# A gated recurrence and its two-layer network: turning the inputs by transposing DMA from DRAM scratch instead of on TensorE, with a set order for every engine

## Chip, cores, metric

One core of one Trainium2 chip. The metric is device microseconds (us) of one execution, median of the fast runs. A run counts as slow when it is over 1.5% above the fastest of the same kernel.

## The reference

```
f = lb + (1 - lb) * sigmoid(f_logit)          # x, f_logit: 4 x 6144 x 256, fp32
h[t] = f[t] * h[t-1] + (1 - f[t]) * x[t]      # per batch and channel, over 6144 tokens
out = max(h @ w1, h @ w2) @ w_out             # w1, w2: 256 x 1024; w_out: 1024 x 256
```

Both kernels use max(a, b) = a + relu(b - a): "hidden" is relu(h @ (w2 - w1)), and "project" adds h @ (w1 @ w_out), whose weights (w13) are made once. They work on 48 blocks of 512 tokens, 12 to a batch. The recurrence runs over tokens along the free dimension, so channels must lie on partitions, while the inputs in DRAM have one token a row. Somebody has to turn them.

## The kernel before

Inputs are cast to bf16 by the GpSimd DMA queue on the way into SBUF, and turned on TensorE (PE), 16 transposes of 128x128 a block, spread over the slots of the loop.

```python
for name, src in (("fn", f_logit), ("xn", x)):            # load(c): one or two blocks
    nat = inpool.tile([P, CH // P, D], BF16, name=name)   # inpool: 4 buffers a name
    nc.gpsimd.dma_start(out=nat[:, 0:ni, :],
        in_=src[b, t0 : t0 + nt, :].rearrange("(i p) d -> p i d", p=P))
# ... turn(j, slot): two of these a slot, into PSUM
nc.tensor.transpose(dst[:, h, q * P : (q + 1) * P],
    ins[c][s][:, o * NSB + q, h * P : (h + 1) * P], ident_b[:])
# ... recurrence(j): u = sigmoid(-fT) on ACT; v = u * xT, ff = 1 - (1-lb) u, scan -> y on DVE
# ... the loop
for j in range(NBLK + 1):
    # load(c) of the chunk that starts at block j + 4
    for fc in range(FC):                 # 8 slots
        if j < NBLK:     hidden(j, fc)       # 2 matmuls of 512 columns, relu on ACT
        if j > 0:        project(j - 1, fc)  # 5 matmuls of 256 columns
        if j + 2 < NBLK: turn(j + 2, fc)     # 2 transposes
    if j + 2 < NBLK: recurrence(j + 2)
```

A load of a later chunk needs a free buffer in SBUF, so it waits until an earlier one has been turned.

Of the kernel before, what the change touches and what calls it, by code (L numbers as in the profile page):

```python
# [12 lines left out]
ENG = mybir.EngineType  # L13
P = 128
# [3 lines left out]
def kernel(  # L18
# [9 lines left out]
):  # L28
    nc = tc.nc
# [7 lines left out]
    NSB = TB // P  # L37
    CH = 2 * TB
    assert S % CH == 0
    NBB = S // TB  # L40
    NBLK = B * NBB
    chunks = [(0, 1), (1, 1)] + [(j, 2) for j in range(2, NBLK, 2)]
    home = {j + o: (c, o) for c, (j, n) in enumerate(chunks) for o in range(n)}
# [3 lines left out]
    inpool = ctx.enter_context(tc.tile_pool(name="inp", bufs=4))  # L47
# [4 lines left out]
    ps_t = ctx.enter_context(  # L52
        tc.tile_pool(name="ps_t", bufs=1, space=bass.MemoryType.PSUM)
    )
    ps_d = ctx.enter_context(
        tc.tile_pool(name="ps_d", bufs=3, space=bass.MemoryType.PSUM)
    )
    ps_o = ctx.enter_context(
        tc.tile_pool(name="ps_o", bufs=3, space=bass.MemoryType.PSUM)
    )  # L60

    ident_f = const.tile([P, P], FP32)
    make_identity(nc, ident_f[:])
    ident_b = const.tile([P, P], BF16)
    nc.vector.tensor_copy(out=ident_b[:], in_=ident_f[:])  # L65

# [3 lines left out]
    nc.sync.dma_start(out=lbc[:], in_=lower_bound.rearrange("(h p) -> p h", p=P))  # L70
    nc.vector.tensor_scalar(
        out=om[:], in0=lbc[:], scalar1=-1.0, scalar2=1.0, op0=ALU.mult, op1=ALU.add
    )
    nc.vector.tensor_scalar_add(out=nom[:], in0=lbc[:], scalar1=-1.0)

    ins = {}

    def load(c):
        j, n = chunks[c]
        b, k = divmod(j, NBB)  # L80
        t0, nt = k * TB, n * TB
        ni = nt // P
        tiles = []
        for name, src in (("fn", f_logit), ("xn", x)):
            nat = inpool.tile([P, CH // P, D], BF16, name=name)
            nc.gpsimd.dma_start(  # L86
                out=nat[:, 0:ni, :],
                in_=src[b, t0 : t0 + nt, :].rearrange("(i p) d -> p i d", p=P),
            )
            tiles.append(nat)  # L90
        ins[c] = tiles

    ys = {}
    turned = {}

    def turn(j, slot):
        c, o = home[j]
        s, q = divmod(slot, FC // 2)
        if q == 0:
            turned[j, s] = ps_t.tile([P, KC, TB], BF16, name=("fT", "xT")[s])  # L100
        dst = turned[j, s]
        for h in range(KC):
            nc.tensor.transpose(  # L103
                dst[:, h, q * P : (q + 1) * P],
                ins[c][s][:, o * NSB + q, h * P : (h + 1) * P],
                ident_b[:],
            )

    def recurrence(j):
        fT, xT = turned[j, 0], turned[j, 1]  # L110
        prev = ys.get(j - 1) if j % NBB else None
        u = midpool.tile([P, KC, TB], BF16, name="u")
        nc.scalar.activation(out=u[:], in_=fT[:], func=AF.Sigmoid, scale=-1.0)  # L113
        v = midpool.tile([P, KC, TB], BF16, name="v")
        nc.vector.tensor_tensor(out=v[:], in0=u[:], in1=xT[:], op=ALU.mult)  # L115
        ff = midpool.tile([P, KC, TB], BF16, name="ff")
        y = ypool.tile([P, KC, TB], BF16, name="y")
        for h in range(KC):
            nc.vector.tensor_scalar(  # L119
                out=ff[:, h, :],  # L120
                in0=u[:, h, :],
                scalar1=nom[:, h : h + 1],
                scalar2=1.0,
                op0=ALU.mult,
                op1=ALU.add,
            )
            nc.vector.tensor_tensor_scan(  # L127
                out=y[:, h, :],
                data0=ff[:, h, :],
                data1=v[:, h, :],  # L130
                initial=0.0 if prev is None else prev[:, h, TB - 1 : TB],
                op0=ALU.mult,
                op1=ALU.add,
            )
        ys[j] = y

    def weight_prep():
        w1n = wpool.tile([P, KC, DFF], FP32)
        w2n = wpool.tile([P, KC, DFF], FP32)
        wob = wpool.tile([P, FC, D], BF16)  # L140
        w1b = wpool.tile([P, KC, DFF], BF16)
        wdf = wpool.tile([P, KC, DFF], FP32)
        wd = wpool.tile([P, KC, DFF], BF16)
        for g in range(2):
            cols = slice(g * DFF // 2, (g + 1) * DFF // 2)
            for w, src in ((w1n, moe_w1), (w2n, moe_w2)):
                nc.scalar.dma_start(
                    out=w[:, :, cols],
                    in_=src[:, cols].rearrange("(kc p) f -> p kc f", p=P),
                )  # L150
        nc.gpsimd.dma_start(
            out=wob[:], in_=moe_w_out.rearrange("(fc p) c -> p fc c", p=P)
        )
        for g in range(2):
            cols = slice(g * DFF // 2, (g + 1) * DFF // 2)
            nc.scalar.copy(out=w1b[:, :, cols], in_=w1n[:, :, cols])  # L156
            nc.vector.tensor_tensor(  # L157
                out=wdf[:, :, cols],
                in0=w2n[:, :, cols],
                in1=w1n[:, :, cols],  # L160
                op=ALU.subtract,
            )
            for kc in range(KC):
                nc.vector.tensor_scalar_mul(
                    out=wd[:, kc, cols], in0=wdf[:, kc, cols], scalar1=om[:, kc : kc + 1]
                )
        w1T = wpool.tile([P, FC, D], BF16)
        for kc in range(KC):
            for g in range(FC // 4):
                pt = ps_d.tile([P, TB], BF16, name="dT")  # L170
                for q in range(4):
                    fc = 4 * g + q
                    nc.tensor.transpose(
                        pt[:, q * P : (q + 1) * P],
                        w1b[:, kc, fc * P : (fc + 1) * P],
                        ident_b[:],
                    )
                nc.scalar.copy(
                    out=w1T[:, 4 * g : 4 * g + 4, kc * P : (kc + 1) * P],
                    in_=pt[:].rearrange("p (q d) -> p q d", q=4),  # L180
                )
        w13 = wpool.tile([P, KC, D], BF16)
        for kc in range(KC):
            psw = ps_o.tile([P, 2, D], FP32, name="psO")
            for fc in range(FC):
                nc.tensor.matmul(  # L186
                    psw[:, 0, :],
                    lhsT=w1T[:, fc, kc * P : (kc + 1) * P],
                    rhs=wob[:, fc, :],
                    start=(fc == 0),  # L190
                    stop=(fc == FC - 1),
                )
            nc.scalar.mul(w13[:, kc, :], psw[:, 0, :], om[:, kc : kc + 1])
        return wd, wob, w13
# [3 lines left out]
    def hidden(j, fc):  # L198
        y = ys[j]
        dT = ps_d.tile([P, TB], FP32, name="dT")  # L200
        for kc in range(KC):
            nc.tensor.matmul(  # L202
                dT[:],
                lhsT=wd[:, kc, fc * P : (fc + 1) * P],
                rhs=y[:, kc, :],
                start=(kc == 0),
                stop=(kc == KC - 1),
            )
        rt = rpool.tile([P, TB], BF16, name="rt")
        nc.scalar.activation(out=rt[:], in_=dT[:], func=AF.Relu)  # L210
        rts[j, fc] = rt

    pos = {}

    def project(j, slot):
        i, half = divmod(slot, 2)
        g, r = divmod(i, 2)
        y = ys[j]
        if r == 0 and half == 0:
            pos[j] = ps_o.tile([P, 2, D], FP32, name="psO")  # L220
        ps = pos[j]
        tok = slice(i * P, (i + 1) * P)
        steps = [(y[:, kc, tok], w13[:, kc, :]) for kc in range(KC)]
        steps += [(rts[j, fc][:, tok], wob[:, fc, :]) for fc in range(FC)]
        n = len(steps)
        for s in range(half * n // 2, (half + 1) * n // 2):
# [8 lines left out]
        if r == 1 and half == 1:  # L235
            osb = opool.tile([P, 2, D], FP32, name="osb")
            nc.vector.tensor_copy(out=osb[:], in_=ps[:])  # L237
            r0 = j * TB + 2 * g * P
            nc.sync.dma_start(
                out=out[r0 : r0 + 2 * P, :].rearrange("(r p) d -> p r d", p=P),  # L240
                in_=osb[:],
            )

    started = {c: chunks[c][0] for c in range(len(chunks))}
    ahead = 4
    for c in range(len(chunks)):
        if started[c] < ahead:
            load(c)
    for slot in range(FC):
        turn(0, slot)  # L250
    recurrence(0)
    wd, wob, w13 = weight_prep()
    for slot in range(FC):
        turn(1, slot)
# [45 lines left out]
```

## Time and profile before

| | before |
|---|---|
| time, median | 445.1 us (445.04 to 445.15, 2 runs) |
| span of the profiled run | 443.3 us |
| PE busy | 423.0 us, 95% |
| ACT, DVE busy | 63%, 56% |
| moved by DMA | 53.5 MB, 121 GB/s |

The profile's page gives busy time by engine, then the span in 40 slices (9 is busy at 90% or more; PEclk is the granted TensorE clock in tenths; GB/s is what the DMA engines moved, counted at the destination), the DMA queues, and the chain of waits that ended last.

```profile
PE 423.0 (95%) x3488; PEld 309.8 (70%) x3488; DVE 247.0 (56%) x345; ACT 278.5 (63%) x442; POOL 44.9 (10%) x57
...
PE   0689999999999999999999999999999999999996
...
PEclk9999999999999999999999999999999999999999
...
GB/s 221 198 198 215 138 124 152 83 146 123 94 140 127 91 163 94 123 151 87 146 119 99 140 121 96 163 95 124 149 85 149 120 95 48 72 49 71 57 64 95
...
q0 software_dynamic: 50992, 25.69, 46.1%
q1 hardware_dynamic: 26384, 25.17, 18.4%
...
PE 94%; DMA 4%; POOL 1%; DVE 0%; issue 0%; POOLq 0%
PE psO L227 47%; PE dT L202 37%; PE xT L103 5%; PE fT L103 5%; DMA wob<-in_moe_w_out_dram 4%; POOL fn L86 1%; POOL xn L86 1%; PE psO L186 0%; DVE osb L237 0%; POOL ident_f masks.py:199 0%; POOL ident_f masks.py:197 0%; POOLq masks.py:199 0%
```

PE is the bound: 94% of the chain, of which L103, the transposes, is 10%. q0 is the GpSimd queue with the casting loads.

The timeline (start, duration, engine, line, what) shows what a transpose costs. First a slot in the middle of the run, then two slots at the end, where nothing is left to turn.

```profile
200.17 0.59 PE L202 MATMUL dT<-y,wd 128*128 128x512 bf16 x2
...
201.15 0.27 PE L103 MATMUL xT<-ident_b,xn 128*128 128x128 bf16 x2
...
201.26 0.59 PE L202 MATMUL dT<-y,wd 128*128 128x512 bf16 x2
```

```profile
425.94 0.59 PE L202 MATMUL dT<-y,wd 128*128 128x512 bf16 x2
...
426.91 0.59 PE L202 MATMUL dT<-y,wd 128*128 128x512 bf16 x2
```

The hidden matmuls (L202) come every 1.09 us in the first and every 0.98 us in the second: 8.72 us against 7.83 us for a block of eight slots. PE streams without a gap in both, so turning costs 0.89 us a block on the critical chain.

### The profile page before, as it was taken

The numbers are of one execution on the slowest core, as the hardware profiler recorded it, in microseconds if no ns is written. First come the engines' busy times: TensorE is split into PE (matmuls) and PEld (weight loads), VectorE is DVE, ScalarE is ACT, GpSimd is POOL, SyncE is SP. The second block draws the span as 40 slices with busy tenths as digits, with TensorE's granted clock in tenths as the row PEclk, the third lists the DMA queues.
The fourth block names the chain that finished last, engine by engine and source line by source line (L and its number), as shares of the span: only waits on it lengthen the run. The fifth ranks groups of instructions, "written<-read, shape, count | busy, mean of one in ns | idle before, by whom it ended". The sixth has DMA issues, their size and how long they took to land.

```text
span 443.3 us, 8434 instructions
## 1 busy us (share of the span) xinstructions
PE 423.0 (95%) x3488; PEld 309.8 (70%) x3488; DVE 247.0 (56%) x345; ACT 278.5 (63%) x442; POOL 44.9 (10%) x57
## 2 busy tenths in 40 slices
PE   0689999999999999999999999999999999999996
PEld 0567777777777777777777777777777777777765
DVE  2744665565556546655655565466546655654631
ACT  3666666666666766666666666666766666666661
POOL 6300101001001001010010010010100100000000
PEclk9999999999999999999999999999999999999999
DMA  8999769487487495694874965956948731212112
GB/s 221 198 198 215 138 124 152 83 146 123 94 140 127 91 163 94 123 151 87 146 119 99 140 121 96 163 95 124 149 85 149 120 95 48 72 49 71 57 64 95
DMA packets 78501, 53.49 MB, mean 121 GB/s; under 512 B 2688, under 2 KB 77440, under 8 KB 78464
## 3 DMA queue, kind: packets, MB, share of 16 engines
q0 software_dynamic: 50992, 25.69, 46.1%
q1 hardware_dynamic: 26384, 25.17, 18.4%
q10 hardware_dynamic: 1088, 2.10, 1.5%
q8 instruction: 27, 0.44, 0.4%
q14 instruction: 10, 0.08, 0.1%
HBM read 53.48 MB, written 25.17 MB: 177 GB/s over the span
## 4 chain that ended last, share of the span: by engine, by line
PE 94%; DMA 4%; POOL 1%; DVE 0%; issue 0%; POOLq 0%
PE psO L227 47%; PE dT L202 37%; PE xT L103 5%; PE fT L103 5%; DMA wob<-in_moe_w_out_dram 4%; POOL fn L86 1%; POOL xn L86 1%; PE psO L186 0%; DVE osb L237 0%; POOL ident_f masks.py:199 0%; POOL ident_f masks.py:197 0%; POOLq masks.py:199 0%; POOLq L284 0%
## 5 line engine op out<-in xcount | busy, mean ns | idle before, releaser
L210 ACT ACTIVATE rt<-dT 128x512 bf16<-128x512 f32 x384 | 226.8, 597 | 142.2 <-PE dT L202 142.1
L227 PE MATMUL psO<-wob,rt 128*128 128x256 bf16 x1536 | 229.8, 273 | 0.0
L202 PE MATMUL dT<-y,wd 128*128 128x512 bf16 x768 | 228.2, 379 | 1.1 <-DVE y L127 1.1
L227 PEld LDWEIGHTS <-rt 128*128 128x128 bf16 x1536 | 150.3, 98 | 57.5
L237 DVE COPY osb<-psO 128x512 f32<-128x512 f32 x96 | 66.4, 692 | 152.5 <-PE psO L227 152.5
L127 DVE TENSOR_TENSOR_SCAN y<-ff,y,v 128x512 bf16<-128x512 bf16 x88 | 108.2, 1272 | 1.5
L227 PE MATMUL psO<-w_182,y 128*128 128x256 bf16 x384 | 73.3, 273 | 0.0
L227 PEld LDWEIGHTS <-y 128*128 128x128 bf16 x384 | 37.6, 98 | 44.4
L103 PE MATMUL fT<-ident_b,fn 128*128 128x128 bf16 x384 | 52.2, 221 | 13.4 <-DVE ident_b L65 13.4
L202 PEld LDWEIGHTS <-wd 128*128 128x128 bf16 x768 | 59.6, 98 | 0.9 <-DVE y L127 0.5
L103 PE MATMUL xT<-ident_b,xn 128*128 128x128 bf16 x384 | 52.2, 221 | 0.0
L113 ACT ACTIVATE u<-fT 128x1024 bf16<-128x1024 bf16 x48 | 49.1, 1024 | 4.9 <-PE fT L103 2.3
L103 PEld LDWEIGHTS <-fn 128*128 128x128 bf16 x384 | 37.3, 99 | 19.2 <-DMA fn<-in_f_logit_dram 11.0
L86 POOL DMA_DIRECT2D fn<-in_f_logit_dram x25 | 21.9, 874 | 237.0 <-PE fT L103 174.2
L119 DVE TENSOR_SCALAR ff<-u,nom 128x512 bf16<-128x512 bf16 x96 | 29.9, 354 | 25.6 <-ACT u L113 25.6
L103 PEld LDWEIGHTS <-xn 128*128 128x128 bf16 x384 | 37.4, 99 | 4.8
L115 DVE TENSOR_TENSOR v<-u,xT 128x1024 bf16<-128x1024 bf16 x48 | 32.5, 677 | 3.9 <-PE xT L103 3.9
L86 POOL DMA_DIRECT2D xn<-in_x_dram x25 | 21.6, 866 | 68.2 <-PE dT L202 64.9
L127 DVE TENSOR_TENSOR_SCAN y<-ff,v 128x512 bf16<-128x512 bf16 x8 | 9.4, 1211 | 0.1
L157 DVE TENSOR_TENSOR wdf<-w2n,w1n 128x1024 f32<-128x1024 f32 x2 | 2.5, 1226 | 6.5 <-DMA w2n<-in_moe_w_dram 6.5
L156 ACT CAST w1b<-w1n 128x1024 bf16<-128x1024 f32 x2 | 2.1, 1045 | 4.6 <-DMA w1n<-in_moe_w_dram 4.6
L186 PE MATMUL psO<-wob,w1T 128*128 128x256 bf16 x16 | 1.9, 272 | 1.8 <-DMA wob<-in_moe_w_out_dram 1.8
(18 smaller groups left out, 15.2 us busy)
## 6 DMA issues: line engine op xcount, KB each, us to landing
out_dram<-osb SPq DMA_DIRECT2D x96, 256.0 KB, 2.7
fn<-in_f_logit_dram POOLq DMA_DIRECT2D x23, 512.0 KB, 8.2
xn<-in_x_dram POOLq DMA_DIRECT2D x23, 512.0 KB, 8.4
w1n<-in_moe_w_dram ACTq DMA_DIRECT2D x2, 512.0 KB, 6.2
w2n<-in_moe_w_dram ACTq DMA_DIRECT2D x2, 512.0 KB, 7.4
fn<-in_f_logit_dram POOLq DMA_DIRECT2D x2, 256.0 KB, 10.3
xn<-in_x_dram POOLq DMA_DIRECT2D x2, 256.0 KB, 10.9
wob<-in_moe_w_out_dram POOLq DMA_DIRECT2D x1, 512.0 KB, 17.0
```

The lines of the kernel that those rows point to most:

```text
L86: nc.gpsimd.dma_start(out=nat[:, 0:ni, :], in_=src[b, t0 : t0 + nt, :].rearrange("(i p) d -> p i d", p=P),)
L103: nc.tensor.transpose(dst[:, h, q * P : (q + 1) * P], ins[c][s][:, o * NSB + q, h * P : (h + 1) * P], ident_b[:],)
L113: nc.scalar.activation(out=u[:], in_=fT[:], func=AF.Sigmoid, scale=-1.0)
L115: nc.vector.tensor_tensor(out=v[:], in0=u[:], in1=xT[:], op=ALU.mult)
L119: nc.vector.tensor_scalar(out=ff[:, h, :], in0=u[:, h, :], scalar1=nom[:, h : h + 1], scalar2=1.0, op0=ALU.mult, op1=ALU.add,)
L127: nc.vector.tensor_tensor_scan(out=y[:, h, :], data0=ff[:, h, :], data1=v[:, h, :], initial=0.0 if prev is None else prev[:, h, TB - 1 : T ...
L156: nc.scalar.copy(out=w1b[:, :, cols], in_=w1n[:, :, cols])
L157: nc.vector.tensor_tensor(out=wdf[:, :, cols], in0=w2n[:, :, cols], in1=w1n[:, :, cols], op=ALU.subtract,)
L202: nc.tensor.matmul(dT[:], lhsT=wd[:, kc, fc * P : (fc + 1) * P], rhs=y[:, kc, :], start=(kc == 0), stop=(kc == KC - 1),)
L210: nc.scalar.activation(out=rt[:], in_=dT[:], func=AF.Relu)
L227: nc.tensor.matmul(ps[:, r, :], lhsT=steps[s][0], rhs=steps[s][1], start=(r == 0 and s == 0), stop=(r == 1 and s == n - 1), skip_group_che ...
L237: nc.vector.tensor_copy(out=osb[:], in_=ps[:])
```

## The change

Intent: take the turning off PE. The first 4 blocks are loaded as fp32 on the SP queue, gated with tokens still on partitions, and turned on PE as before. For the other 44, a pair of blocks at a time: GpSimd's queue casts f_logit and x to bf16 into DRAM scratch, and SP's queue loads them with a transposing DMA, channels on partitions. The order of every engine's instructions is set by hand, the weights' preparation is rewritten, and an output tile takes tokens 2p and 2p+1 to partition p, so that a store writes 2 KB runs and projection reads its weights at a step of two.

```diff
-            nc.gpsimd.dma_start(out=nat[:, 0:ni, :], in_=src[b, t0 : t0 + nt, :]...)
+    scratch = tc.tile_pool(name="scratch", bufs=2, space=bass.MemoryType.DRAM)
+    ttpool = tc.tile_pool(name="turned", bufs=3)
+    def cast(c):                                  # c: a pair of blocks
+        for name, src in (("fs", f_logit), ("xs", x)):
+            t = scratch.tile([CB * TB, D], BF16, name=name)
+            nc.gpsimd.dma_start(out=t[:], in_=src[b, k * TB : (k + CB) * TB, :])
+            rows[c].append(t)
+    def turn_dma(c, s):
+        t = ttpool.tile([P, KC, CB * TB], BF16, name=("fT", "xT")[s])
+        nc.sync.dma_start_transpose(out=t[:], in_=rows[c][s][:])
... # opening: direct loads, weights, blocks 0 and 1, with cast(0) and cast(1) in it
+        for j in range(1, NBLK + 1):
+            for fc in range(FC):
+                hidden(j, fc); project(j - 1, fc)              # j = 1 differs
... # blocks 2 and 3: gated, turned on PE, scanned
+                b = j + 2
+                if NP <= b < NBLK:
+                    if fc == 4: gate(b)                        # ACT reads fT
+                    if fc == 5: drive(b), forget and scan      # DVE reads xT
+                if fc == 5 and j % 2 == 1:
+                    c = (j + 3 - NP) // 2
+                    if 0 <= c < NCH:
+                        for s in range(2): turn_dma(c, s)
+                    if c + 2 < NCH:
+                        cast(c + 2)
```

## The prediction

> **What bounds the kernel now.** TensorE. The chain of waits puts 94% of the 443.3 us span on PE: 47% projection matmuls, 37% hidden matmuls, 10% fT and xT transposes. The table by stretches shows PE busy all of 40 to 430 us at clock 1.00. The timeline at 200 us shows hidden, projection and turning matmuls with a period of 1.09 us a slot, 8.72 us a block of eight slots; at 425 us, where nothing is left to turn, the same slots come every 0.98 us, 7.83 us a block. So turning one block costs PE 0.89 us that nothing hides. ACT (63%) and DVE (56%) have slack.
>
> The opening: the first hidden matmul starts at 18.0 us, PE waits 2 us for the cast of w_out (17 us to landing), the steady loop (block 1) starts at 27.2 us. From there 45 x 8.72 + 2 x 7.83 + 4.4 gives 412, as the timeline has it; 4.0 us of copy and last store follow.
>
> **What the change does.**
> - Removes the PE turning of 44 of 48 blocks, about 43 of them in the loop and on the critical chain: 0.89 us each, about 38 us.
> - Adds DMA: per pair of blocks a cast of 2 x 1 MB to scratch and two transposing loads of 512 KB. No trace here shows such a load. The Trainium skill, "DMA: Bandwidth & Descriptors", section Latency and other measured facts, has 261 GB/s for one with a non-contiguous middle dimension; from that, as an estimate, 4 us of data a pair plus some 2 us of latency. A pair has 15.7 us. Casts took 8.4 us to landing with two in flight, stores 2.7 us. DMA share in the steady stretch was 0.7; the opening shows 1.45 reached, so there is room. A load is issued about 7 us before its sigmoid; five PSUM buffers for hidden let PE run about 4 us past a late ACT.
> - Stores become 2 KB runs; projection's weights are read at a step of two. 40 weight loads a block hide behind 109 ns matmuls (transposes show loads every 56 ns): I expect no cost.
> - Opening: block 0 lands as fp32 near 6 us, its scans end near 10, hidden(0) starts at 11, but w_out (fp32, behind 3 MB, then cast on POOL) gates w13 near 18, and block 1's gate sits behind that: scan(1) ends near 26. Half of block 0's projection is done by then.
>
> **Sum (estimate).** Block 1's loop starts at 26; block 1: 6.6; 1 us wait for scan(2); block 2: 8.7; blocks 3 to 47: 45 x 7.83 = 352; last projection 4.4; tail 4. Span 403, time (1.8 us above the span, as before) 404 us, range 398 to 416. Chances: faster by over 2% 0.93, within 2% 0.04, slower 0.03.
>
> **What would show it.** Slots of 0.98 us from block 4 to the end; PE busy total down by about 40 us, 64 bf16 transposes of inputs instead of 768; projection matmuls still 109 ns apart; chain over 90% PE; transposing loads landing within 7 us; ACT's waits in the loop ended by PE, not DMA; block 1's hidden matmuls starting near 26 us.
>
> **What would make it wrong.** Slow transposing loads: at over about 10 us a pair, sigmoid waits for DMA, PSUM fills and PE stalls each pair; if casts, loads and stores together need over 15.7 us, DMA becomes the bound (430 us or more). Step-two weight loads slower than 109 ns add to 1,920 matmuls, 2 us for each ns. The opening loads may hold back the first cast, stalling around 35 to 50 us.

## The result

| | before | after |
|---|---|---|
| time, median | 445.1 us | 530.0 us (527.75 and 532.25) |
| ratio of fast runs | 1 | 1.1905, 95% interval 1.1785 to 1.2025 |
| span of the profiled run | 443.3 us | 526.0 us |
| PE busy | 423.0 us | 399.5 us |
| mean granted clock | 1.00 | 0.875 |

A ratio here is the mean time of one kernel's fast runs over that of the other's of the same rounds, so it is not quite the ratio of the medians quoted.

The page after, same parts:

```profile
PE 399.5 (76%) x2792; PEld 275.4 (52%) x2792; DVE 247.9 (47%) x343; ACT 273.2 (52%) x444; POOL 27.3 (5%) x54
...
PE   5880200140005999999999999999999999999996
...
PEclk8786555575555999999999999999999999999999
...
GB/s 289 332 210 213 212 251 216 197 91 207 105 57 97 139 160 154 128 109 132 131 151 161 137 116 116 133 140 161 140 119 124 121 141 160 143 139 95 138 70 81
DMA packets 112689, 79.11 MB, mean 150 GB/s; under 512 B 94288, under 2 KB 98384, under 8 KB 111952
...
q1 hardware_dynamic: 110976, 55.59, 44.8%
q0 software_dynamic: 1408, 23.07, 21.9%
...
PE 71%; another core or an unknown queue 23%; ACT 2%; DMA 1%; DVE 1%; issue 1%; SPq 0%; POOL 0%; DVEq 0%; POOLq 0%
```

The PE row has a hole from the fourth slice into the thirteenth and is full after it. The chain gives 23% to "another core or an unknown queue". In order of time, that is two pieces:

```profile
38.13 63.44 another core or an unknown queue
...
105.46 56.67 another core or an unknown queue
```

Between 38 and 164 us the core did almost nothing; from there on it works as forecast. This table by stretches has busy time by engine, then the granted clock, the DMA share and GB/s moved:

```profile
38.00:101.00 63.00, 5.29 (x33) 3.21 (x30) 0.13 (x1) 3.09 (x5) 11.72 (x25) 0.56 1.03 222
101.00:164.00 63.00, 8.41 (x46) 5.15 (x46) 5.04 (x6) 2.44 (x4) 2.92 (x6) 0.55 1.11 122
...
200.00:500.00 300.00, 300.00 (x2150) 210.20 (x2149) 192.15 (x268) 211.37 (x346) 0.00 (x0) 1.00 0.53 136
```

So the question is not why transposing loads are slow. In the steady part they are not: the timeline of the SP queue below has a pair every 15.6 us, and the trace's list by tile gives a median of 4.5 us to landing for fT. What the hole waited for is in the table of waits (engine, line, releaser: total us, times, longest):

```profile
DVE vn L106 <- DMA xn<-in_x_dram: 64.7, 3, 63.5
...
DVE v L186 <- DMA xT<-xs: 57.1, 1, 57.1
ACT u L175 <- DMA fT<-fs: 56.7, 1, 56.7
```

Each is in essence one single wait: x of block 3, a plain load issued at 15.35 us, is used at 101.7 us; then the first transposing load, issued at 30.5, at 162. Here is SP's queue around it and in the steady part:

```profile
15.35 1.41 SPq L89 DMA_DIRECT2D xn<-in_x_dram  x1
...
30.51 113.20 SPq L170 DMA_TRANSPOSE fT<-fs  x1
143.81 15.92 SPq L170 DMA_TRANSPOSE xT<-xs  x1
...
201.72 2.10 SPq L170 DMA_TRANSPOSE fT<-fs  x1
203.91 2.40 SPq L170 DMA_TRANSPOSE xT<-xs  x1
...
217.36 2.02 SPq L170 DMA_TRANSPOSE fT<-fs  x1
```

and this is what GpSimd did meanwhile (the first cast, one on the way, and the last):

```profile
16.30 0.67 POOL L164 DMA_DIRECT2D fs<-in_f_logit_dram  x1
...
40.08 0.49 POOL L164 DMA_DIRECT2D fs<-in_f_logit_dram  x1 [2.03 <-DMA fs<-in_f_logit_dram]
...
126.94 0.49 POOL L164 DMA_DIRECT2D xs<-in_x_dram  x1 [1.98 <-DMA xs<-in_x_dram]
```

All 22 pairs of casts were issued between 16 and 127 us, while the loop, whose pass j = 2 holds both waits above, stood still. In the loop a cast stands after the transposing loads of two pairs before, but that is its place in GpSimd's order alone, and GpSimd has nothing else to do. The built program has no wait for anything but an earlier cast. These are two of its instruction rows for GpSimd (the waits are on the semaphores of the software DMA queue):

```
13 L164 DMACopy fs<-in_f_logit_dram 16x16384
21 L164 DMACopy fs<-in_f_logit_dram 16x16384 [waits DMASW0_49]
```

The pool's "bufs=2" gives no wait either. An SBUF pool hands its buffers out in turn and makes the next writer wait; here no cast waits for the loads that read scratch before, and since kernels with the casts as far ahead as here (e2 and e10 below) give correct results, the scratch tiles do not share memory.

Two more facts. The page's 23.07 MB in 1,408 packets is a mean of 16.4 KB, but no cast packet has that size: only 737 packets of the whole run are 8 KB or larger. The trace's packet records, which the page sums up, have 704 cast packets of 32,768 bytes, 16 to a cast, and 704 of four bytes. (The "16 KB" of the expectations below is this mean.) A plain load has packets of 1 KB and a transposing one of 256 bytes, 2,048 for each of the 44 loads. And between 38 and 101 us the casts, two of 0.52 MB every 5.04 us, moved 208 of the 222 GB/s, which leaves 14 for all else, the loads that everyone waited for among it.

### The profile page after: what moved, and what is told of

Its sections match the earlier page's. It is cut to its first block, busy times and chain, and to the rows that moved or that the text cites. A ratio compares the mean times of both kernels' runs of the same rounds, so it can differ in the third digit from the quotient of the medians.

```text
span 526.0 us, 7133 instructions
## 1 busy us (share of the span) xinstructions
PE 399.5 (76%) x2792; PEld 275.4 (52%) x2792; DVE 247.9 (47%) x343; ACT 273.2 (52%) x444; POOL 27.3 (5%) x54
## 3 DMA queue, kind: packets, MB, share of 16 engines
q0 software_dynamic: 1408, 23.07, 21.9%
## 4 chain that ended last, share of the span: by engine, by line
PE 71%; another core or an unknown queue 23%; ACT 2%; DMA 1%; DVE 1%; issue 1%; SPq 0%; POOL 0%; DVEq 0%; POOLq 0%
PE psO L229 39%; PE dT L200 31%; DMA w2n<-in_moe_w_dram 1%; ACT wd L269 1%; PE dT L118 0%; DVE vn L106 0%; ACT rt L212 0%; SPq L89 0%; POOL wdf L263 0%; PE psO L292 0%; DVE osb L240 0%; DVE y L147 0%; ACT u L175 0%; ACT un L99 0%
## 5 line engine op out<-in xcount | busy, mean ns | idle before, releaser
L212 ACT ACTIVATE rt<-dT 128x512 bf16<-128x512 f32 x380 | 220.9, 596 | 155.9 <-PE dT L200 155.6
L200 PE MATMUL dT<-y,wd 128*128 128x512 bf16 x768 | 232.4, 386 | 4.3 <-DVE y L147 2.2
L186 DVE TENSOR_TENSOR v<-u,xT 128x1024 bf16<-128x1024 bf16 x44 | 30.5, 692 | 116.4 <-ACT u L175 59.3
L200 PEld LDWEIGHTS <-wd 128*128 128x128 bf16 x768 | 75.8, 99 | 17.6 <-issue 4.3
L175 ACT ACTIVATE u<-fT 128x1024 bf16<-128x1024 bf16 x44 | 46.1, 1048 | 56.7 <-DMA fT<-fs 56.7
L229 PE MATMUL psO<-w,y 128*128 128x256 bf16 x384 | 74.1, 275 | 0.0
L106 DVE TENSOR_TENSOR vn<-un,xn 128x1024 bf16<-128x1024 bf16 (+1 forms) x5 | 5.1, 1012 | 68.9 <-DMA xn<-in_x_dram 64.7
L118 PE MATMUL dT<-ident_b,un 128*128 128x128 bf16 x32 | 3.1, 246 | 21.2 <-ACT un L99 21.2
L99 ACT ACTIVATE un<-fn 128x1024 bf16<-128x1024 f32 (+1 forms) x5 | 4.4, 882 | 23.3 <-DMA fn<-in_f_logit_dram 23.3
L164 POOL DMA_DIRECT2D fs<-in_f_logit_dram x22 | 10.9, 495 | 53.7 <-DMA fs<-in_f_logit_dram 53.7
L164 POOL DMA_DIRECT2D xs<-in_x_dram x22 | 10.7, 487 | 35.9 <-DMA xs<-in_x_dram 35.9
L147 DVE TENSOR_TENSOR_SCAN y<-ff,y,dT 128x512 bf16<-128x512 bf16 x6 | 7.4, 1266 | 1.7 <-PE dT L118 1.7
```

The lines of the kernel that those rows point to most:

```text
L106: nc.vector.tensor_tensor(out=vs[j][:, q0:q1, :], in0=us[j][:, q0:q1, :], in1=ins[j][1][:, q0:q1, :], op=ALU.mult,)
L118: nc.tensor.transpose(dst[:, h, q * P : (q + 1) * P], src[:, q, h * P : (h + 1) * P], ident_b[:])
L147: nc.vector.tensor_tensor_scan(out=ys[j][:, h, :], data0=ffs[j][:, h, :], data1=vT[j][:, h, :], initial=0.0 if prev is None else prev[:, h ...
L164: nc.gpsimd.dma_start(out=t[:], in_=src[b, k * TB : (k + CB) * TB, :])
L175: nc.scalar.activation(out=us[j][:], in_=chunk[c, 0][:, :, o * TB : (o + 1) * TB], func=AF.Sigmoid, scale=-1.0,)
L186: nc.vector.tensor_tensor(out=vT[j][:], in0=us[j][:], in1=chunk[c, 1][:, :, o * TB : (o + 1) * TB], op=ALU.mult,)
```

## The experiments

Theory A: the casts run ahead of the loop because nothing holds them, and their large packets leave the loads a small share of each DMA engine. The Trainium skill, "DMA: Bandwidth & Descriptors", section Queues, rings and completion order, says that each engine goes round the queue rows at the granularity of a packet, draining a whole one before it switches. One packet of 1 KB for each cast packet, 16.4 KB in the mean of large and four-byte ones, would be 208 x 1/16.4 = 13 GB/s. The packet records agree: between 60 and 80 us they have 128 cast packets of 32,768 bytes, 128 of four bytes, and 255 load packets of 1 KB, one for one, which is 13.1 GB/s for the load. Rivals: B, a transposing load is slow beside any traffic; C, casts that run ahead use up the bandwidth whatever their packets.

### e1: casts paced by block

```diff
+    pace = const.tile([P, 1], BF16)
...
                     if c + 2 < NCH:
+                        nc.gpsimd.tensor_copy(out=pace[:], in_=rts[j, 5][:, 0:1])
                         cast(c + 2)
```

> One edit: before casts 2 to 21, GpSimd copies one element of the rectified tile of block j, so a cast can't be issued before block j is reached; packets stay as they are (16 KB mean). Theory A (casts run ahead of the schedule, since nothing in the program makes a cast wait for its turn, and their 16 KB packets leave loads of 256 B and 1 KB packets a small share of each DMA engine): the 126 us hole between 38 and 164 us goes; casts spread over the span; about 405 to 420 us, with transposing loads that run beside a cast landing in 8 to 11 us instead of 4.5. Theory B (a transposing load is slow beside any other traffic, whoever issues it): the hole turns into a stall in each pair of blocks, transposing loads landing in over 15 us, time over 480 us.

Correct. Four runs, 473.5 to 491.2 us, of which only the fastest counts as fast; before, 445.1. The hole is gone, and the stalls came back spread out: too slow for A, and yet fT landed in 8.1 us by the median, not B's 15 (in a profile of a slow run). B's time, over 480 us, fits the three slow runs and not the fast one. Both were wrong about something.

### e2: casts in small packets, not paced

```diff
-            nc.gpsimd.dma_start(out=t[:], in_=src[b, k * TB : (k + CB) * TB, :])
+            nc.gpsimd.dma_start(
+                out=t[:].rearrange("(i p) d -> p i d", p=P),
+                in_=src[b, k * TB : (k + CB) * TB, :].rearrange("(i p) d -> p i d", p=P))
```

> One edit: each cast is issued with rows of one token (1 KB read, 512 B written) in an order that can't be merged, so its packets are 512 B instead of 16 KB; casts still run ahead, up to eight in flight. Theory A by packet share: loads of 1 KB and 256 B get about an even number of packets, so block 3's loads land by about 40 us instead of 101 us, the first transposing load lands in 10 to 20 us instead of 132, time 410 to 435 us. Theory C (the casts that run ahead simply use up HBM or engine bandwidth, whatever the packet size): the hole stays until the last cast has landed near 145 us, time 515 to 535 us.

Correct, 479.5 us (478.5 to 479.6, 4 runs), ratio to before 1.0768, interval 1.0752 to 1.0784. Halfway: no direct x load took over 11.7 us to landing instead of 86.2, no fT over 15.3 us and no xT over 17.9, so the starving went as A says. The time followed neither range: until the last casts land, near 198 us, PE is busy only 62 to 85% of the stretches from 30 us on. With an even share the transposing loads of a pair are still too slow beside up to eight casts in flight.

### e3: paced and small

> Both edits: casts paced and in 512 B packets. Theory A: no load is starved and no cast is early; transposing loads land in 5 to 8 us, block period 7.82 us from block 4, time 402 to 410 us. If it is slower than e1 by over 2 us, small packets cost more than the starving beside 16 KB packets does. Theory C: same as e1 within 1%.

Correct. Four runs, 472.1 to 482.2 us; the two fast ones are 472.1 and 475.3, as e1's fast one (473.5). Theory A's 402 to 410 is far off. With neither backlog nor large packets the two fast runs are still 27 and 30 us over before. The profile (of a fast run) says where: first GpSimd's casts, then SP's transposing loads, then the waits.

```profile
203.50 0.87 POOL L165 DMA_DIRECT2D fs<-in_f_logit_dram  x1
204.36 0.87 POOL L165 DMA_DIRECT2D xs<-in_x_dram  x1
```

```profile
206.88 7.49 SPq L174 DMA_TRANSPOSE fT<-fs  x1
214.45 3.87 SPq L174 DMA_TRANSPOSE xT<-xs  x1
```

```profile
DVE v L190 <- DMA xT<-xs: 102.0, 15, 10.6
ACT u L179 <- DMA fT<-fs: 60.1, 11, 8.5
```

A transposing load that meets a cast holds SP for 7.49 us instead of 2.1. Over the run such loads took up to 13.4 (fT) and 14.0 us (xT) to landing, and ACT and DVE waited for them 11 and 15 times. Pacing by block puts a cast exactly beside the loads it stands next to in the program. The packet records show that such a load is late to start: fT, issued at 206.88 us, moved its first packet 5.6 us later, against 1.4 us for an fT that meets no cast (208.17 us in e5). Theory D: the two in flight together slow each other, and each fits when they are apart.

### e4: one pair of casts for all

```diff
         rows[c] = []
+        if c > 0:
+            rows[c] = rows[0]
+            return
```

> Wrong result on purpose: only the first pair of blocks is cast, and all transposing loads read that scratch. It takes 42 of 44 casts away and leaves all else. Theories A and C: the hole goes, no contention left, 400 to 407 us; what it is above my 404 is then the mis-sized opening, not the DMA. Theory B: as slow as after where transposing loads meet the stores, over 480 us.

Wrong result. 407.0 us (406.1 to 407.8, 4 runs), ratio 0.9144. fT took at most 5.8 us and xT 6.1 beside the stores. Theory B is out, and so is any fault of the loop, the stores, or the step-two weight loads: without casts the changed kernel is 3 us from the forecast.

### e5: casts and transposing loads apart

One line against the changed kernel, plus the tile it writes. The copy reads an element of xT, so GpSimd can't issue the next casts before that load has landed (it is the second of the pair; fT, issued some 2 us before it, had landed by then too, as its at most 6.5 us show).

```diff
+    pace = const.tile([P, 1], BF16)
...
                     if c + 2 < NCH:
+                        nc.gpsimd.tensor_copy(out=pace[:], in_=chunk[c, 1][:, 0, 0:1])
                         cast(c + 2)
```

> Casts 2 to 21 are each held, by a one-element GpSimd copy, until the transposing loads of the pair before have landed, so that a cast and a transposing load are in flight at different times. Theory D (a cast and a transposing load in flight together slow each other, above all the load; each fits in the 15.6 us of a pair when they are apart): transposing loads land in 4.2 to 6 us as in e4, DVE and ACT do not wait for DMA in the loop, 405 to 412 us. Theory C2 (the DMA engines have too little capacity for 3.15 MB moved a pair, however it is arranged): 440 us or more, transposing loads late since casts land late.

Correct, 407.7 us (406.5 to 408.0, 5 runs), ratio to before 0.9149, interval 0.9136 to 0.9163. Cast packets are as large as in the changed kernel, and all 44 casts are made. Its page, then SP's and GpSimd's order:

```profile
PE 391.1 (96%) x2792; PEld 272.1 (67%) x2792; DVE 248.0 (61%) x343; ACT 273.4 (67%) x444; POOL 31.3 (8%) x74
...
PE   5679999999999999999999999999999999999996
...
GB/s 242 397 242 251 109 211 191 199 211 187 225 186 181 206 190 212 222 221 184 218 182 199 243 166 203 251 161 208 203 206 205 190 183 246 160 113 157 55 90 91
...
q0 software_dynamic: 1408, 23.07, 29.6%
...
PE 93%; DMA 2%; ACT 1%; DVE 1%; issue 1%; SPq 1%; POOL 0%; DVEq 0%; POOLq 0%
```

```profile
208.17 2.07 SPq L171 DMA_TRANSPOSE fT<-fs  x1
...
210.34 2.33 SPq L171 DMA_TRANSPOSE xT<-xs  x1
...
214.87 0.19 POOL L414 COPY pace<-xT 128x1 bf16<-128x1 bf16 x1 [14.58 <-DMA xT<-xs]
...
215.68 0.49 POOL L165 DMA_DIRECT2D fs<-in_f_logit_dram  x1 [0.62 <-issue]
...
223.25 3.01 SPq L171 DMA_TRANSPOSE fT<-fs  x1
```

```profile
100.00:200.00 100.00, 100.00 (x719) 70.13 (x718) 64.25 (x89) 70.21 (x115) 8.25 (x21) 1.00 0.91 202
```

The pair of loads issued at 208.2 us has landed at 214.9; only then are the casts issued, and the next pair of loads follows at 223.3. fT took at most 6.5 us, PE is busy 100 of every 100 us, and the slots come every 0.98 us. This is theory D's number, with 202 GB/s moved; capacity (C2) is not the limit when the transfers are apart.

How much room is left can be worked out. A pair of blocks writes 1.05 MB of scratch, 1.05 MB of turned input and 1.05 MB of output; in 15.64 us that is 201 GB/s, what e5 moved. While e2's casts were in flight (60 to 170 us) the engines moved 198 to 206 GB/s, and PE was busy 67% of the time. That is not the most the engines can do: they moved 222 in the changed kernel's hole, and 397 in the second slice of e5's opening, with other kinds of transfers. So neither the share nor GB/s alone says whether there is room; e2 and e5 moved the same and differ in what was in flight together. How much slack e5's order leaves is not shown.

### e7: loads a pair earlier, casts beside them

```diff
-                    c = (j + 3 - NP) // 2
+                    c = (j + 5 - NP) // 2     # at j = 1: pairs 0 and 1, and casts 2 and 3
```

with e1's pacing.

> Casts paced by block as in e1, colliding with the transposing loads, but these are issued one pair of blocks earlier (23 us before their sigmoid instead of 7). Theory D with enough capacity: the loads are still slow (8 to 19 us) but in time, so 405 to 415 us. Theory C2: moving the loads earlier helps little, 440 us or more.

Correct; 408.7, 417.1, 423.6 and 433.4 us. One run counts as fast. It is as good as e5, so a load that comes early enough may be slow; but the other three are late by 8 to 25 us, so with casts beside the loads it does not hold reliably. The profiled run is the slowest one (433.4), and its trace shows most of the lateness: ACT and DVE waited for a transposing load only once, 1.0 us, but two such loads held SP's queue for 16.95 us (from 189.4) and 16.67 us (from 210.3), and the stores share that queue. The output copy on DVE waited 22.8 us, until 225.3, for a store to land and free its buffer, and PE 17.4 us for that copy. That the held queue made the store late is the likely reading, not a tested one. The other two slow runs have no trace here.

### e8: apart and a pair earlier

e7's order of loads with e5's pacing.

> Both: casts apart from transposing loads, and these issued one pair earlier. Theory D: 404 to 410 us, at most 3 us better than e5. Theory C2: 440 us or more.

Correct, 407.9 us (407.3 to 408.9, 4 runs), ratio 0.9165. The same time as e5, but its transfers were not apart:

```profile
203.61 0.49 POOL L165 DMA_DIRECT2D xs<-in_x_dram  x1
```

```profile
207.37 5.32 SPq L171 DMA_TRANSPOSE fT<-fs  x1
```

With the loads a pair earlier, fT was issued while the casts were still in flight, in nearly every pair; it landed in 8.9 us by the median (4.8 in e5) and moved its first packet, here, 4.6 us after its issue. ACT and DVE did not wait for it in the loop. So e8 shows, as e7's fast run does, that a slowed load can cost nothing when it comes a pair earlier. That 7 us ahead is enough when the transfers are apart is shown by e5.

### e9 and e10: is it the packet?

Both start from the changed kernel, casts not paced. e9 gives the direct loads of blocks 1 to 3 runs of 4 KB (wrong result), e10 gives the casts runs of 4 KB.

```diff
-                "(q p) d -> p q d", p=P                                      # e9
+                "(p q) d -> p q d" if j else "(q p) d -> p q d", p=P
-            nc.gpsimd.dma_start(out=t[:], in_=...)                           # e10
+            nc.gpsimd.dma_start(
+                out=t[:].rearrange("(i p q) d -> p i (q d)", p=16, q=8),
+                in_=at.rearrange("(i p q) d -> p i (q d)", p=16, q=8))
```

> Wrong result on purpose (tokens of blocks 1 to 3 in another order): in the changed kernel, the direct loads of blocks 1 to 3 take 4 KB a partition in one run instead of four of 1 KB; casts unpaced and in 16 KB packets as before. Theory A (DMA engines take turns by packet): these loads get four times the share beside the casts, about 44 instead of 14 GB/s, so x of block 3 lands near 45 us on the clock instead of 101; the hole's first part (38 to 101 us) goes, its second, the starved transposing loads of 256 B packets, stays until the casts end near 145: 510 to 530 us. If the turn is not by packet, x of block 3 stays near 100 us.

> Casts unpaced, but in runs of eight tokens (8 KB read, 4 KB written) instead of 32 KB and more. Theory A by packet: x of block 3 (landing 86 us after its issue with 16 KB packets, at most 12 us with 512 B) lands some 25 to 45 us after its issue; the first transposing load, of 256 B packets, in 50 to 110 us (132 and 15 before); time between 479 and 530 us. If size does not matter but only the run structure of e2 does, it is like e2.

| run | large cast packets | direct load packet | slowest x load to landing | slowest fT load to landing | time |
|---|---|---|---|---|---|
| after | 32.8 KB | 1 KB | 86.2 us | 131.6 us | 530.0 us |
| e9 | 32.8 KB | 4 KB | 29.5 us | 102.6 us | 500.0 us |
| e10 | 4.1 KB | 1 KB | 26.2 us | 52.5 us | 499.6 us |
| e2 | 0.5 KB | 1 KB | 11.7 us | 15.3 us | 479.5 us |

(Sizes are those of the trace's packet records; in each run 704 of the queue's 1,408, 6,336 or 45,760 packets are of four bytes.) Four times larger load packets, with the casts untouched, bring x of block 3 in by 43 us on the clock, near the 45 that A gave; casts of 4 KB do nearly the same from the other side. e10 was inside its ranges. e9's time was not: 500 instead of 510 to 530, since its casts ended earlier (last pair issued near 111 us, not 127). The packet records have the turns one for one again: 736 packets of each queue between 43 and 100 us in e9, 1,237 of each between 61 and 84 us in e10. So the packet-share part of A is shown at three sizes of one side and two of the other, for the direct loads and for the transposing loads of e9 and e10. The fT column says less in two rows: in the changed kernel and in e9 fT landed just after the last cast packet ended (162.1 against 161.8 us, 133.8 against 132.3), so its time there is set by the casts' end. In the second piece of the changed kernel's hole the turns are not one for one (125 to 145 us: 169 cast packets, 663 of fT), and why is open.

## Why the prediction was wrong

It said 404 us, and the kernel took 530. Point by point:

- **What turning costs, and what removing it is worth: right.** It gave 0.89 us for about 43 blocks, 38 us. e5, which does all of the change's work, has a span of 405.9 against 443.3, that is 37.4 us less; slots of 0.98 us, PE at 93% of the chain. That 37.4 is so near 38 is partly luck, since the sum had 40 with a gain in the opening that did not come; and PE's busy total fell by 31.9 us, not 40, for the new opening keeps PE busier (29.1 against 23.7 us of the first 40).
- **Speed of a transposing load: right where no cast is beside it.** Landing in 7 us was forecast; e5 and the steady part of the changed kernel have 4.4 to 4.8 us by the median. From the Trainium skill's 261 GB/s the prediction estimated 4 us of data a pair; in e5 the packets of the pair issued at 208.2 us moved from 209.6 to 214.2 us, 4.6 us or 226 GB/s, and issue to landing took 6.7 us.
- **No cost of step-two weight loads: right.** A weight load takes 98 ns in e5 as before, a projection matmul 273 ns in both. The Trainium skill, "TensorE: Matmul & The Clock Gate", section Weight-path perf modes, lists packed or strided reads for its fast weight load; the trace agrees in that the step of two cost nothing, but does not show whether these loads are the fast ones.
- **The step that failed:** "Adds DMA: per pair of blocks a cast of 2 x 1 MB to scratch and two transposing loads of 512 KB. ... A pair has 15.7 us." This spreads the casts evenly, one pair of them to one pair of blocks. In the program nothing does: up to eight are in flight from 16 us on, and 22 pairs were issued before block 4 could start. The text even named the place, "stalling around 35 to 50 us", but had the direct loads hold back the cast; the runs show the casts holding back the direct loads, then the first transposing load, for 120 us of chain (63.4 + 56.7). Taking the casts away (e4) or holding them (e5) gives 407. The same line also took it that a cast and a load can be in flight together and still fit: "4 us of data a pair plus some 2 us of latency". With the casts spread as the line has them (e3), fT landed in 6.7 and xT in 9.4 us by the median and in up to 14.0, often later than the 7 us that a load is issued ahead, and the kernel took 472.1 us in its fastest run. So two things failed, the pace of the casts and their overlap with the loads.
- **"DMA share in the steady stretch was 0.7; the opening shows 1.45 reached, so there is room": not shown by that number.** Share counts the time of packets, which overlap; e2 shows 1.35 with 198 to 206 GB/s moved and PE starved, and e5 runs at 0.91 with 202 GB/s and PE full. There was room, as e5 and e8 show, for casts kept apart from the loads or loads issued a pair earlier. Pacing alone (e1, e3) recovered about half of the 126 us: a spread-out cast still met the loads, and the load came later than the 7 us and some slack that it had.
- **The opening: forecast at 26 us, measured later.** Block 1's hidden matmuls start at 28.3 us after and 29.0 in e5, against 27.0 before (the prediction read 27.2), so the new opening gains only the half of block 0's projection done by then. Part of the slip is at its start: hidden(0) was to start at 11 us and started at 13.2 (13.9 in e5), having waited for the scaled weights from ACT. In e5 block 2 starts at 36.9 us, where the sum had 26 + 6.6 + 1 = 33.6; that accounts for the 3 us by which e5's span of 405.9 exceeds the 403 forecast.

What is shown: that held casts restore the forecast, that packet size on either side sets how long a starved direct load takes, and that casts beside transposing loads cost time even when paced. Not shown: why a transposing load beside a paced cast is slow. Turn-taking by packet alone does not account for it: in e3, beside cast packets of 0.5 KB that took some 60 ns each by the median, the load's first packet came 5.6 us after its issue. And e1 and e3, with 32.8 KB and 0.5 KB packets, have about the same fast times, as far as one and two fast runs can say, so packet size is not the whole of it.

The cold clock (PEclk 5 in the hole) followed from the hole: the Trainium skill, same TensorE page, Part 1, has half clock after idle windows, the trace 0.55 to 0.56 there and 0.93 on average from 164 to 200 us.

## What to carry to other kernels

An instruction's place in the program paces nothing on an engine that has no other work: when a buffer's reuse was what made a producer wait, and the change takes that wait away, look at the built program for what it waits on now, and put in a wait that is meant. Put background transfers where the critical ones are not (here one copied element a pair of blocks took 530 us to 408, and it beats both kernels), and remember that a bulk copy with large packets beside small-packet loads does not share evenly with them. A load that holds its queue also holds the stores behind it (in the changed kernel the next store was issued at 159.8 us). Before saying that there is room, ask which transfers will be in flight together: e2 and e5 moved the same 200 GB/s or so, one with PE busy 67% of the time, the other 100%.

## What the Trainium skill lacked or had wrong

- "DMA: Bandwidth & Descriptors", Queues, rings and completion order, states the turn-taking by packet, but not what it does to a load: with DRAM-to-DRAM cast packets of 32.8 KB, a 512 KB load of 1 KB packets took 86.2 us, and a transposing load, of 256-byte packets, 131.6 us, against 11.7 and 15.3 us with casts of 0.5 KB. Nor does it say why a transposing load beside a paced cast starts late (5.6 us to its first packet in e3 against 1.4 in e5).
- The same page tells authors of kernels that "A transpose next to ordinary DMAs needs nothing". For correct results the runs agree; for time, a transposing load took up to 14.0 us beside a paced cast (e3) and at most 6.5 us apart from it (e5).
- The same page gives bandwidth for a transposing DMA, and sequencer cycles for one of small tiles, but not what a large one holds of its issuing queue: 2.1 us of SP for a load of 1024 x 256 bf16, 7.5 us beside a cast, 113 us beside the backlog (the next store is issued at 159.8 us).
- No page says that casting copies from DRAM to DRAM come in packets of 32.8 KB (with one of four bytes for each) when both sides are contiguous, and of 0.5 KB when written as rows of one token.
